# Window attention and a two-layer FFN on one core: TensorE's operands placed at multiples of 64 bytes, and the 512-column products of the second layer issued as two of 256

## The chip, the cores and the metric

The kernel runs on one core of a Trainium2 chip. The metric is the device time of one execution in microseconds (us), lower is better. The kernel before took 1079.14 us as the median of three runs (1075.65 to 1079.49).

## The reference

Windowed attention with 32 global tokens for 8 batches of 8 heads, whose output is the input of a feed-forward network with a squared ReLU. Cut to what matters:

```
s_g   = scale * q_g @ [k_g, k_l].T          # 32 global queries, 544 keys
out_g = softmax(s_g) @ [v_g, v_l]
s_l   = scale * q_l @ [k_g, k_l].T          # 512 local queries, keys within 32 places
out_l = softmax(mask(s_l)) @ [v_g, v_l]
x = concat(out_g, out_l) as (4608, 512)     # head_dim 64, 8 heads
h = x @ w_in                                # (512, 2048)
g = s * relu(h)**2 + b
out = g @ w_out                             # (2048, 512), all float32
```

## The kernel before, in words

**Precision.** A float32 operand is split into two float32r parts, a rounded one and the rest, and each product is made of three: high by high, high by low, low by high. TensorE reads 4 bytes an element in all of them.

**Attention.** Work goes in 128 steps j, one for a batch, a half of the queries and a head. The scores (`scores`, line 376) are products with 192 or 224 moving columns; `softmax` runs on VectorE and ScalarE; the probabilities are transposed on TensorE (line 317) and multiplied with the values (line 403); the global queries take lines 382, 455 and 477. The first 16 steps (`NF`) run in plain float32 on lines 283, 291, 317 and 341, while the weights of the network arrive and are split into `w_all` (lines 146 to 160).

**The network.** A tile t is 256 rows of x; 17 tiles of 8 steps make 136 steps m, and step m runs 10 steps (`LAG`) behind attention. `ffn_in` (line 525) makes two blocks of 128 hidden columns with 24 products: stationary operand 128 columns of `w_all`, moving operand 256 columns of `xs` (the split x). ScalarE and VectorE make `g` from them (lines 531 to 540). `ffn_out` (line 557) makes 12 products: stationary 128 columns of `g`, moving 512 columns of `w_all`, summed over 8 steps into two PSUM tiles `acc`. So every step m costs TensorE 24 products of 256 columns and 12 of 512, and each product loads its own stationary operand (the rows PEld of a profile).

**Order.** The program is written step by step and then put in order by the tile framework's scheduler, which goes by a simulated timeline; what stands in each engine's queue is the scheduler's choice, and small pieces of one product group can be put between two pieces of another.

**Where the operands lie.** The pools `const` and `sb` lay their tiles one behind the other in each SBUF partition, in the order of their first use, each padded to a multiple of 32 bytes. In the built program `w_all` starts at byte 2560, which is 40 times 64. Behind it the 4 bytes of `unread` take 32, and the tiles that follow start 32 bytes past a multiple of 64: `xs` at 141728 and 149920, `vs` at 158112, `sm` at 164384, `pt` at 171936, `kq` at 178592, `g` at 205344 and 209440, `qgs` at 213664, `pg` at 215712, `vsg` at 223392. Slices of these tiles start at multiples of 64 bytes from the tile's start. So each product of the network has one operand on a multiple of 64 and one off it: on line 525 the stationary `w_all` is on and the moving `xs` off, on line 557 the moving `w_all` is on and the stationary `g` off. In the products of attention (lines 376, 382, 403, 477) both operands are off. For the transposes the moving `ident` (1152) is on and the stationary `sm` off.

Of the kernel before, what the change touches and what calls it, by code (L numbers as in the profile page):

```python
# [10 lines left out]
F32 = mybir.dt.float32  # L11
F32R = mybir.dt.float32r
# [10 lines left out]
P = 128  # L23
# [49 lines left out]
def window_attention_then_ffn(ctx: ExitStack, tc: tile.TileContext, qd, qg, kw, vw, vg, qz, qgz, vz, w_in, w_out, sv, bv, out):  # L73
    nc = tc.nc
    scale = 1.0 / math.sqrt(D)

    const = ctx.enter_context(tc.tile_pool(name="const", bufs=1))
    sb = ctx.enter_context(tc.tile_pool(name="sb", bufs=2))
    ps = ctx.enter_context(tc.tile_pool(name="ps", bufs=1, space=bass.MemoryType.PSUM))

    dram = ctx.enter_context(tc.tile_pool(name="dram", bufs=1, space=bass.MemoryType.DRAM))

    ident = const.tile([P, P], F32, name="ident")
    make_identity(nc, ident)
    s_t = const.tile([P, 1], F32, name="s_t")
    b_t = const.tile([P, 1], F32, name="b_t")
# [11 lines left out]
    keep_busy(WARM_FIRST, "warm0")  # L98


    masks = {}
    for first, parts in ((True, ((32, 192, 0),)), (False, ((0, 160, 0), (192, 224, 32)))):
        mask = const.tile([P, 192 if first else 224], BF16, name=f"mask{int(first)}")
        nc.gpsimd.memset(mask, 0.0)

        for c0, c1, skip in parts:
            for sign, base in ((1, c0 - skip), (-1, 64 - c0 + skip)):
                nc.gpsimd.affine_select(
                    out=mask[:, c0:c1], in_=mask[:, c0:c1], pattern=[[sign, c1 - c0]], compare_op=ALU.is_ge,
                    fill=NEG, base=base, channel_multiplier=-sign,  # L110
                )
        masks[first] = mask


    w_all = const.tile([P, 2, 16, 2, DM], F32R, name="w_all")
    wi = w_all[:, :, :, 0].rearrange("p a f (c q) -> p a f c q", c=4)
    wo = w_all[:, :, :, 1]

# [6 lines left out]
    nc.scalar.activation(out=unread, in_=warm[:, 0:1], func=AF.Exp)  # L125

    def weight_chunk(k):
        st = sb.tile([P, 2048], I32, tag=SPOTS[k], name=f"wst{k}", bufs=2)
        n = 2 if k < BY_HALVES else 1
        sources = (w_in[k], w_out[k * P:(k + 1) * P, :])  # L130
        for i in range(2):
            queue = nc.scalar if k == 0 else nc.sync
            queue.dma_start(st[:, 1024 * i:1024 * (i + 1)], sources[i])
        for i in range(n):
            c = 1024 // n
            weight_words(k, st[:, 2 * c * i:2 * c * (i + 1)], slice(c * i, c * (i + 1)))

    def weight_words(k, st, at):
        words = st.rearrange("p (n w) -> p n w", w=2)
        low, high = words[:, :, 0], words[:, :, 1]  # L140
        n = at.stop - at.start
        parts = [slice(c, c + 512) for c in range(0, n, 512)]
        ups = []
        for h in parts:
            up = sb.tile([P, 512], I32, tag="vs", name=f"wup{k}_{at.start + h.start}", bufs=2)
            nc.scalar.activation(out=up, in_=low[:, h].bitcast(U32), func=AF.Copy, scale=2.0**-29)
            ups.append(up)
        nc.scalar.activation(out=low.bitcast(F32), in_=high.bitcast(F32), func=AF.Copy, scale=2.0**-112)  # L148
        nc.vector.tensor_scalar(
            out=low, in0=low, scalar1=3, scalar2=0x7FFFFFFF, op0=ALU.logical_shift_left, op1=ALU.bitwise_and,  # L150
        )
        for h, up in zip(parts, ups):
            nc.vector.tensor_tensor(out=low[:, h], in0=low[:, h], in1=up, op=ALU.add)  # L153
# [6 lines left out]
        nc.vector.tensor_sub(out=lo, in0=m, in1=f32(hi))  # L160
# [24 lines left out]
    def split(j):  # L185
        b, hf, h = slot(j)
        rk, rq = st_.pop(("rk", j)), st_.pop(("rq", j))
        p0 = 64 * (h % 2)
        p1 = 64 - p0
        if h % 2 == 0:  # L190
            st_["kq", j] = st_["kq", j + 1] = sb.tile([P, 2048], F32R, tag="kq", name=f"kq{j}", bufs=2)
        kq = st_.pop(("kq", j))[:, 1024 * (h % 2):1024 * (h % 2) + 1024]
        ks, qs = kq[:, 0:NC], kq[:, 512:1024].rearrange("p (i q) -> p i q", i=2)
        nc.scalar.copy(out=ks[p0:p0 + 64], in_=rk[p0:p0 + 64])  # L194
        (nc.gpsimd if K_POOL(j) else nc.vector).tensor_sub(out=ks[p1:p1 + 64], in0=rk[p0:p0 + 64], in1=f32(ks[p0:p0 + 64]))  # L195
        nc.scalar.copy(out=qs[:, 0, :], in_=rq)  # L196
        nc.gpsimd.tensor_sub(out=qs[:, 1, :], in0=rq, in1=f32(qs[:, 0, :]))  # L197
        st_["ks", j], st_["qs", j] = kq[:, 0:480], qs

    def v_split(j):  # L200
        rv = st_.pop(("rv", j))
        vs = sb.tile([P, 4, 2, D], F32R, tag="vs", name=f"vs{j}", bufs=2)
        rv4 = rv.rearrange("p (c d) -> p c d", d=D)
        nc.scalar.copy(out=vs[:, :, 0, :], in_=rv4)  # L204
        nc.gpsimd.tensor_sub(out=vs[:, :, 1, :], in0=rv4, in1=f32(vs[:, :, 0, :]))  # L205
        st_["vs", j] = vs

    def softmax(j, p_s):
        b, hf, h = slot(j)
        sm = sb.tile([P, NC], F32, tag="sm", name=f"sm{j}")  # L210
        nm = sb.tile([P, 2], F32, tag="nm", name=f"nm{j}")
        ss = sb.tile([P, 2], F32, tag="ss", name=f"ss{j}")
        cols = [COLS[hf, blk] for blk in range(2)]
        for blk in range(2):
            c = cols[blk]
            mask = masks[hf == 0 and blk == 0][:, 0:c.stop - c.start]
            nc.vector.tensor_tensor_reduce(  # L217
                out=sm[:, c], in0=p_s[:, c], in1=mask,
                op0=ALU.add, op1=ALU.min, scale=-scale, scalar=BIG, accum_out=nm[:, blk:blk + 1],
            )  # L220
        for blk in range(2):
            p = sm[:, cols[blk]]
            nc.scalar.activation(  # L223
                out=p, in_=p, func=AF.Exp, bias=nm[:, blk:blk + 1], scale=-1.0, accum_out=ss[:, blk:blk + 1],
            )
        nc.vector.tensor_scalar_add(ss, ss, 1e-9)
        nc.vector.reciprocal(ss, ss)
        for blk in range(2):
            p = sm[:, cols[blk]]
            if NORM_ACT(j):  # L230
                nc.scalar.activation(out=p, in_=p, func=AF.Copy, scale=ss[:, blk:blk + 1])  # L231
            else:
                nc.vector.tensor_scalar(  # L233
                    out=p, in0=p, scalar1=ss[:, blk:blk + 1], scalar2=1.0, op0=ALU.mult, op1=ALU.mult,
                )
        st_["p", j] = sm
# [84 lines left out]
    def transposes32(j):  # L321
        list(p_transposes(j))
        p_t = st_.pop(("pst", j))
        if j % 2 == 0:
            st_["ptp", j + 1] = sb.tile([P, 2, NC], F32, tag="pt", name=f"pt{j}")
        pt = st_["ptp", j + 1 - j % 2][:, j % 2]
        nc.scalar.copy(out=pt, in_=p_t)
        st_["pt", j] = pt
# [32 lines left out]

    def qg_split(b):
        rqg = st_["rqg", b].rearrange("p (h q) -> p h q", h=H)
        qgs = sb.tile([P, H, 2, SG], F32R, tag="qgs", name=f"qgs{b}", bufs=1)
        nc.scalar.copy(out=qgs[:, :, 0, :], in_=rqg)
        nc.gpsimd.tensor_sub(out=qgs[:, :, 1, :], in0=rqg, in1=f32(qgs[:, :, 0, :]))
        st_["qgs", b] = qgs
# [20 lines left out]

    def p_split(j):
        p_t = st_.pop(("pst", j))  # L390
        pt = sb.tile([P, 2, NC], F32R, tag="pt", name=f"pt{j}")
        nc.scalar.copy(out=pt[:, 0], in_=p_t)  # L392
        nc.vector.tensor_sub(out=pt[:, 1], in0=p_t, in1=f32(pt[:, 0]))
        st_["pt", j] = pt
# [67 lines left out]
    def g_load(b, h):  # L462
        rv = sb.tile([P, 10 * D], F32, tag="rvg", name=f"rvg{b}_{h}", bufs=1)
        nc.sync.dma_start(rv, vg[b, h // 2])
        vs = sb.tile([P, 2, 5, 2, D], F32R, tag="vsg", name=f"vsg{b}_{h}", bufs=1)
        for i in range(2):
            rv5 = rv[:, 5 * D * i:5 * D * (i + 1)].rearrange("p (c d) -> p c d", d=D)
            nc.scalar.copy(out=vs[:, i, :, 0, :], in_=rv5)  # L468
# [21 lines left out]
    xs_ = {}  # L490

    def x_split(t):
        xs = sb.tile([P, 2, 4, HALF], F32R, tag="xs", name=f"xs{t}", bufs=2)
        x = xcur.pop(t)
        for i in range(2):
            v = slice(2 * i, 2 * i + 2)
# [2 lines left out]
        xs_[t] = xs  # L499

    def xg_split(t):
        xs = sb.tile([P, 2, 4, HALF], F32R, tag="xs", name=f"xs{t}", bufs=2)
        for i in range(2):
            xr = sb.tile([P, DM], F32, tag="r", name=f"xgr{i}", bufs=2)
            nc.sync.dma_start(xr, xg_d[i * P:(i + 1) * P, :])
# [10 lines left out]
    def ffn_in(m):  # L516
# [13 lines left out]
        r = sb.tile([P, 2, HALF], F32, tag="r", name=f"r{m}", bufs=2)  # L530
        nc.scalar.activation(out=r, in_=p_h, func=AF.Relu)  # L531
        nc.vector.scalar_tensor_tensor(out=r, in0=p_h, scalar=s_t, in1=r, op0=ALU.mult, op1=ALU.mult)  # L532
        g = sb.tile([P, 2, 2, HALF], F32R, tag="g", name=f"g{m}")
        if GL_POOL(m):
            nc.vector.tensor_scalar_add(r, r, b_t)
            nc.scalar.copy(out=g[:, 0], in_=r)
# [10 lines left out]
    def ffn_out(m):  # L547
# [4 lines left out]
        for i in range(2):  # L552
            n = 0
            for k in range(2):
                f = 2 * pr + k
                for a, e in ((0, 0), (0, 1), (1, 0)):
                    nc.tensor.matmul(  # L557
                        oacc[t][i], lhsT=g[:, a, k, i * P:(i + 1) * P], rhs=wo[:, e, f, :],
                        start=(pr == 0 and n == 0), stop=(pr == 7 and n == 5),
                    )  # L560
# [169 lines left out]
```

## Time and profile before

| | |
|---|---|
| median of three runs | 1079.14 us (1075.65 to 1079.49) |
| the profiled execution | 1075.98 us, its span 1074.2 us |
| granted TensorE clock, mean | 0.985 |
| PE busy | 1034.1 us (96%), 7100 products |
| PEld busy (loads of the stationary operand) | 930.5 us (87%) |
| VectorE busy | 815.6 us (76%) |
| ScalarE busy | 726.6 us (68%) |
| GpSimd busy | 314.7 us (29%) |
| HBM traffic | 82 GB/s over the span |

The profile is one execution. PE are TensorE's products, PEld the loads of their stationary operands, DVE is VectorE, ACT ScalarE, POOL GpSimd, SP the engine that issues most transfers. A product that starts before the one ahead of it has left the array overlaps it, so its mean length is longer than its share of the time; the pace of a group is read from the starts: from the start of a group to the start of the next one, divided by the number of products. Times within the profile count from the span's start.

### The profile page before, as it was taken

Reading aid. Unit: us, or ns where it says so; the run is one execution under the profiler, and the core shown is the slowest. Engines: PE = TensorE matmul, PEld = TensorE weight load, DVE = VectorE, ACT = ScalarE, POOL = GpSimd, SP = SyncE. Lnnn points to the kernel's source line nnn. Section 1 sums busy time; section 2 is a strip of 40 time slices with the busy share of each in tenths; the row PEclk is TensorE's granted clock in tenths of the full one; section 3 lists DMA queues with packets and bytes.
Section 4 is the critical chain, followed back from the end, with each engine's and each line's share of the span. In section 5 each row is a group of like instructions: output and inputs, shape, how many; then the busy total and the mean of one; then the engine's idle time right before and its main releaser. Section 6 shows DMA issues by size and latency. Waiting matters only on the chain.

```text
span 1074.2 us, 20403 instructions
## 1 busy us (share of the span) xinstructions
PE 1034.1 (96%) x7100; PEld 930.5 (87%) x7100; DVE 815.6 (76%) x2069; ACT 726.6 (68%) x1821; POOL 314.7 (29%) x365
## 2 busy tenths in 40 slices
PE   8789779999999999999999999999999999999996
PEld 4578568999999999999999999999999999999895
DVE  5878885887879877897879887997789788963321
ACT  6898685775867776785778676876678676743221
POOL 1000161432434323442334242432344233301000
PEclk9999879999999999999999999999999999999999
DMA  7765431221313222321223131312232122201000
GB/s 258 231 192 185 144 100 49 86 76 38 101 52 101 61 66 64 92 77 46 83 69 106 38 98 55 107 57 71 59 91 77 46 89 69 68 1 47 22 20 20
DMA packets 63535, 88.89 MB, mean 83 GB/s; under 512 B 7624, under 2 KB 48584, under 8 KB 63432
## 3 DMA queue, kind: packets, MB, share of 16 engines
q1 hardware_dynamic: 63144, 86.54, 25.8%
q8 instruction: 56, 0.92, 0.3%
q10 hardware_dynamic: 288, 1.05, 0.3%
q14 instruction: 47, 0.39, 0.1%
HBM read 78.12 MB, written 9.44 MB: 82 GB/s over the span
## 4 chain that ended last, share of the span: by engine, by line
PE 81%; DVE 7%; ACT 6%; DMA 4%; issue 1%; POOL 0%; SPq 0%; ACTq 0%; POOLq 0%; DVEq 0%
PE acc L557 33%; PE ps_h L525 31%; PE ps_t L317 4%; PE ps_o L403 4%; PE ps_s L376 4%; DMA wst<-in_w_in 2%; PE ps_og L477 2%; PE ps_g L382 1%; ACT sm L223 1%; DVE sm L233 1%; DVE w_all L160 1%; DMA wst<-in_w_out 1%; DVE wst L153 1%; PE ps_tg L455 1%; ACT wst L148 1%
## 5 line engine op out<-in xcount | busy, mean ns | idle before, releaser
L525 PE MATMUL ps_h<-xs,w_all 128*128 128x256 f32 x3264 | 448.8, 284 | 8.1 <-DVE w_all L160 3.8
L525 PEld LDWEIGHTS ps_h<-xs,w_all 128*128 128x128 f32 x3264 | 417.1, 190 | 20.5 <-DVE w_all L160 4.6
L557 PE MATMUL acc<-w_all,g 128*128 128x512 f32 x1632 | 430.1, 400 | 0.4 <-ACT g L539 0.3
L557 PEld LDWEIGHTS acc<-w_all,g 128*128 128x128 f32 x1632 | 291.0, 189 | 54.8 <-ACT g L539 0.7
L197 POOL TENSOR_TENSOR kq<-rq,kq 128x256 fp32r<-128x256 f32 x112 | 98.3, 878 | 233.4 <-ACT kq L196 216.8
L205 POOL TENSOR_TENSOR vs<-rv,vs 128x256 fp32r<-128x256 f32 x112 | 85.6, 765 | 269.4 <-ACT vs L204 258.6
L532 DVE SCALAR_TENSOR_TENSOR r<-ps_h,s_t,r 128x512 f32<-128x512 f32 x136 | 101.4, 745 | 64.6 <-ACT r L531 64.5
L531 ACT ACTIVATE r<-ps_h 128x512 f32<-128x512 f32 x136 | 81.2, 598 | 86.7 <-PE ps_h L525 79.1
L223 ACT ACTIVATE sm<-sm,nm 128x224 f32<-128x224 f32 (+1 forms) x256 | 118.6, 467 | 18.9 <-DVE nm L217 17.6
L540 DVE SCALAR_TENSOR_TENSOR g<-r,b_t,g 128x512 fp32r<-128x512 f32 x136 | 106.6, 784 | 31.7 <-ACT g L539 27.5
L539 ACT ACTIVATE g<-r,b_t 128x512 fp32r<-128x512 f32 x136 | 98.7, 726 | 43.4 <-DVE r L532 42.5
L217 DVE CUSTOM_DVE_ANT_0 sm<-ps_s,mask 128x224 f32<-128x224 f32 (+1 forms) x256 | 85.3, 368 | 27.0 <-PE ps_t L317 14.8
L317 PE MATMUL ps_t<-ident,sm 128*128 128x128 f32 x512 | 95.2, 279 | 5.2 <-ACT sm L231 4.6
L233 DVE TENSOR_SCALAR sm<-sm,ss 128x192 f32<-128x192 f32 (+1 forms) x224 | 83.2, 411 | 3.3
L469 POOL TENSOR_TENSOR vsg<-rvg,vsg 128x320 fp32r<-128x320 f32 x64 | 56.8, 906 | 96.4 <-ACT vsg L468 96.3
L403 PE MATMUL ps_o<-pt,vs 128*128 128x256 f32 x448 | 84.1, 283 | 0.0
L376 PE MATMUL ps_s<-kq 128*128 128x192 f32 (+1 forms) x448 | 77.9, 279 | 5.0 <-DVE kq L195 2.7
L376 PEld LDWEIGHTS ps_s<-kq 128*128 128x128 f32 x448 | 68.8, 193 | 12.3 <-ACT sm L223 2.4
L386 ACT COPY tg<-ps_g 32x256 f32<-32x256 f32 (+1 forms) x112 | 42.3, 378 | 50.1 <-PE ps_g L382 47.6
L392 ACT CAST pt<-ps_t 128x416 fp32r<-128x416 f32 x112 | 57.3, 512 | 24.8 <-PE ps_t L317 24.1
L195 POOL TENSOR_TENSOR kq<-rk,kq 64x416 fp32r<-64x416 f32 x56 | 66.9, 1194 | 21.8 <-ACT kq L194 15.9
L403 PEld LDWEIGHTS ps_o<-pt,vs 128*128 128x128 f32 x448 | 67.6, 193 | 2.5 <-POOL vs L205 0.2
(73 smaller groups left out, 1235.0 us busy)
## 6 DMA issues: line engine op xcount, KB each, us to landing
rq<-in_qd SPq DMA_DIRECT2D x112, 128.0 KB, 2.0
rv<-in_vw SPq DMA_DIRECT2D x112, 128.0 KB, 2.0
rk<-in_kw SPq DMA_DIRECT2D x64, 208.0 KB, 2.4
rvg<-in_vg SPq DMA_DIRECT2D x32, 320.0 KB, 2.9
out<-o SPq DMA_DIRECT2D x34, 256.0 KB, 2.3
wst<-in_w_in SPq DMA_DIRECT2D x15, 512.0 KB, 4.0
wst<-in_w_out SPq DMA_DIRECT2D x15, 512.0 KB, 5.4
rv<-in_vz SPq DMA_DIRECT2D x16, 256.0 KB, 2.9
```

Of the source, the lines that this page charges most:

```text
L197: nc.gpsimd.tensor_sub(out=qs[:, 1, :], in0=rq, in1=f32(qs[:, 0, :]))
L205: nc.gpsimd.tensor_sub(out=vs[:, :, 1, :], in0=rv4, in1=f32(vs[:, :, 0, :]))
L223: nc.scalar.activation(out=p, in_=p, func=AF.Exp, bias=nm[:, blk:blk + 1], scale=-1.0, accum_out=ss[:, blk:blk + 1],)
L233: nc.vector.tensor_scalar(out=p, in0=p, scalar1=ss[:, blk:blk + 1], scalar2=1.0, op0=ALU.mult, op1=ALU.mult,)
L317: nc.tensor.transpose(out=p_t[:, at:at + P], in_=sm[:, c0:c0 + P], identity=ident)
L376: nc.tensor.matmul(p_s[:, cols], lhsT=qs[:, a, blk * P:(blk + 1) * P], rhs=ks[:, cols], start=(a == 0), stop=(a == 1),)
L403: nc.tensor.matmul(p_o[:, blk, :, q0:q0 + n], lhsT=vs[:, 2 * blk + c], rhs=pt[:, :, o], start=(c == 1), stop=(c == 0),)
L525: nc.tensor.matmul(p_h[:, k], lhsT=wi[:, a, f, c], rhs=xs[:, e, c, :], start=(n == 0), stop=(n == 11),)
L532: nc.vector.scalar_tensor_tensor(out=r, in0=p_h, scalar=s_t, in1=r, op0=ALU.mult, op1=ALU.mult)
L539: nc.scalar.activation(out=g[:, 0], in_=r, func=AF.Identity, bias=b_t)
L540: nc.vector.scalar_tensor_tensor(out=g[:, 1], in0=r, scalar=b_t, in1=f32(g[:, 0]), op0=ALU.add, op1=ALU.subtract,)
L557: nc.tensor.matmul(oacc[t][i], lhsT=g[:, a, k, i * P:(i + 1) * P], rhs=wo[:, e, f, :], start=(pr == 0 and n == 0), stop=(pr == 7 and n == 5),)
```

## The change

Three things are done.

1. A new pool `ops`, opened ahead of the others, takes the tiles that TensorE reads in the steady part: `ident`, one mask, `w_all`, `xs` (and `wst`), `vs` (and `wup`), `sm`, `pt`, `kq`, `g`, `qgs`, `vsg`. Their sizes are all multiples of 64 bytes, so in the built program all of them start at a multiple of 64: `w_all` at 2048, `xs` at 133120 and 141312, `vs` at 149504, `sm` at 153600, `pt` at 156928, `kq` at 163584, `g` at 179968 and 184064, `qgs` at 188160, `vsg` at 190208. The numbers of buffers stay what they were. The tiles left in `sb` stay 32 bytes past a multiple of 64, among them `pg` (220832), the stationary operand of line 477, and the float32 tiles `rk`, `rq`, `rv` and `sg`.
2. Each product of `ffn_out` with 512 moving columns becomes two with 256, one behind the other, with the same stationary operand; line 557 becomes line 559 and goes from 1632 products to 3264. Each of the two loads the stationary operand again.
3. As the program and its simulated times differ, the scheduler puts the instructions in another order.

```
+    ops = ctx.enter_context(tc.tile_pool(name="ops", bufs=1))
+    ident = ops.tile([P, P], F32, name="ident")
+    masks = {first: ops.tile([P, 192 if first else 224], BF16, name=f"mask{int(first)}") for first in (True,)}
+    w_all = ops.tile([P, 2, 16, 2, DM], F32R, name="w_all")
...
+    masks[False] = const.tile([P, 224], BF16, name="mask0")
...
-        vs = sb.tile([P, 4, 2, D], F32R, tag="vs", name=f"vs{j}", bufs=2)
+        vs = ops.tile([P, 4, 2, D], F32R, tag="vs", name=f"vs{j}", bufs=2)
...
-        xs = sb.tile([P, 2, 4, HALF], F32R, tag="xs", name=f"xs{t}", bufs=2)
+        xs = ops.tile([P, 2, 4, HALF], F32R, tag="xs", name=f"xs{t}", bufs=2)
...
-        g = sb.tile([P, 2, 2, HALF], F32R, tag="g", name=f"g{m}")
+        g = ops.tile([P, 2, 2, HALF], F32R, tag="g", name=f"g{m}", bufs=2)
...
                 for a, e in ((0, 0), (0, 1), (1, 0)):
-                    nc.tensor.matmul(
-                        oacc[t][i], lhsT=g[:, a, k, i * P:(i + 1) * P], rhs=wo[:, e, f, :],
-                        start=(pr == 0 and n == 0), stop=(pr == 7 and n == 5),
-                    )
+                    for z in range(2):
+                        at = slice(HALF * z, HALF * (z + 1))
+                        nc.tensor.matmul(
+                            oacc[t][i][:, at], lhsT=g[:, a, k, i * P:(i + 1) * P], rhs=wo[:, e, f, at],
+                            start=(pr == 0 and n == 0 and z == 0), stop=(pr == 7 and n == 5 and z == 1),
+                        )
                     n += 1
```

The same move from `sb` to `ops` is made for `wst`, `wup`, `kq`, `sm`, `pt`, `qgs` and `vsg`.

TensorE's queue in a step in the middle of the program, before. `ps_o` are products of probabilities and values, `ps_t` transposes, `acc_0` and `acc_1` the second layer, `ps_s` and `ps_g` scores, `ps_h` the first layer.

```order
L403 MATMUL ps_o_6055<-pt_5965,vs_5968 128x256
L403 MATMUL ps_o_6055<-pt_5965,vs_5968 128x2x96
L317 MATMUL ps_t_6058<-ident,sm_5906 128x128 x2
L403 MATMUL ps_o_6055<-pt_5965,vs_5968 128x256
L403 MATMUL ps_o_6055<-pt_5965,vs_5968 128x2x64
L317 MATMUL ps_t_6058<-ident,sm_5906 128x128 x2
L557 MATMUL acc_0_5782<-w_all,g_5948 128x512 x6
L557 MATMUL acc_1_5783<-w_all,g_5948 128x512 x6
L376 MATMUL ps_s_6096<-kq_5890 128x224 x2
L376 MATMUL ps_s_6096<-kq_5890 128x192 x2
L382 MATMUL ps_g_6101<-kq_5890,qgs_4450 64x288
L525 MATMUL ps_h_6120<-xs_5583,w_all 128x256 x24
```

And such a step of the changed kernel:

```order
L403 MATMUL ps_o_6554<-pt_6463,vs_6466 128x256
L403 MATMUL ps_o_6554<-pt_6463,vs_6466 128x2x96
L317 MATMUL ps_t_6557<-ident,sm_6404 128x128 x2
L403 MATMUL ps_o_6554<-pt_6463,vs_6466 128x256
L403 MATMUL ps_o_6554<-pt_6463,vs_6466 128x2x64
L317 MATMUL ps_t_6557<-ident,sm_6404 128x128 x2
L559 MATMUL acc_0_6361<-w_all,g_6551 128x256 x12
L559 MATMUL acc_1_6362<-w_all,g_6551 128x256 x12
L376 MATMUL ps_s_6723<-kq_6493 128x224 x2
L376 MATMUL ps_s_6723<-kq_6493 128x192 x2
L382 MATMUL ps_g_6728<-kq_6493,qgs_4885 64x288
L525 MATMUL ps_h_6747<-xs_6138,w_all 128x256 x24
```

The step keeps its order; the two rows of the second layer hold 12 products of 256 columns in place of 6 of 512.

The last steps on TensorE's queue, where attention is over, before:

```order
L525 MATMUL ps_h_13720<-xs_13423,w_all 128x256 x24
L557 MATMUL acc_0_13534<-w_all,g_13705 128x512 x6
L557 MATMUL acc_1_13535<-w_all,g_13705 128x512 x6
L525 MATMUL ps_h_13763<-xs_13423,w_all 128x256 x24
L557 MATMUL acc_0_13534<-w_all,g_13748 128x512 x6
L557 MATMUL acc_1_13535<-w_all,g_13748 128x512 x6
```

And in the changed kernel:

```order
L525 MATMUL ps_h_15319<-xs_14938,w_all 128x256 x24
L559 MATMUL acc_0_15073<-w_all,g_15292 128x256 x12
L559 MATMUL acc_1_15074<-w_all,g_15292 128x256 x12
L525 MATMUL ps_h_15374<-xs_14938,w_all 128x256 x24
L559 MATMUL acc_0_15073<-w_all,g_15347 128x256 x12
L559 MATMUL acc_1_15074<-w_all,g_15347 128x256 x12
```

Here too nothing but the shape and the number of the second layer's products moves.

More of the change, by code (lines that the diff above doesn't have):

```diff
@@ L81, in window_attention_then_ffn @@
     dram = ctx.enter_context(tc.tile_pool(name="dram", bufs=1, space=bass.MemoryType.DRAM))
-    ident = const.tile([P, P], F32, name="ident")
+    masks[False] = const.tile([P, 224], BF16, name="mask0")
     make_identity(nc, ident)
@@ L98, in window_attention_then_ffn @@
     keep_busy(WARM_FIRST, "warm0")
-    masks = {}
     for first, parts in ((True, ((32, 192, 0),)), (False, ((0, 160, 0), (192, 224, 32)))):
-        mask = const.tile([P, 192 if first else 224], BF16, name=f"mask{int(first)}")
+        mask = masks[first]
         nc.gpsimd.memset(mask, 0.0)
@@ L111, in window_attention_then_ffn @@
                 )
-        masks[first] = mask
-    w_all = const.tile([P, 2, 16, 2, DM], F32R, name="w_all")
     wi = w_all[:, :, :, 0].rearrange("p a f (c q) -> p a f c q", c=4)
@@ L127, in weight_chunk @@
     def weight_chunk(k):
-        st = sb.tile([P, 2048], I32, tag=SPOTS[k], name=f"wst{k}", bufs=2)
+        st = ops.tile([P, 2048], I32, tag=SPOTS[k], name=f"wst{k}", bufs=2)
         n = 2 if k < BY_HALVES else 1
@@ L144, in weight_words @@
         for h in parts:
-            up = sb.tile([P, 512], I32, tag="vs", name=f"wup{k}_{at.start + h.start}", bufs=2)
+            up = ops.tile([P, 512], I32, tag="vs", name=f"wup{k}_{at.start + h.start}", bufs=2)
             nc.scalar.activation(out=up, in_=low[:, h].bitcast(U32), func=AF.Copy, scale=2.0**-29)
@@ L190, in split @@
         if h % 2 == 0:
-            st_["kq", j] = st_["kq", j + 1] = sb.tile([P, 2048], F32R, tag="kq", name=f"kq{j}", bufs=2)
+            st_["kq", j] = st_["kq", j + 1] = ops.tile([P, 2048], F32R, tag="kq", name=f"kq{j}", bufs=2)
         kq = st_.pop(("kq", j))[:, 1024 * (h % 2):1024 * (h % 2) + 1024]
@@ L209, in softmax @@
         b, hf, h = slot(j)
-        sm = sb.tile([P, NC], F32, tag="sm", name=f"sm{j}")
+        sm = ops.tile([P, NC], F32, tag="sm", name=f"sm{j}", bufs=2)
         nm = sb.tile([P, 2], F32, tag="nm", name=f"nm{j}")
@@ L324, in transposes32 @@
         if j % 2 == 0:
-            st_["ptp", j + 1] = sb.tile([P, 2, NC], F32, tag="pt", name=f"pt{j}")
+            st_["ptp", j + 1] = ops.tile([P, 2, NC], F32, tag="pt", name=f"pt{j}", bufs=2)
         pt = st_["ptp", j + 1 - j % 2][:, j % 2]
@@ L363, in qg_split @@
         rqg = st_["rqg", b].rearrange("p (h q) -> p h q", h=H)
-        qgs = sb.tile([P, H, 2, SG], F32R, tag="qgs", name=f"qgs{b}", bufs=1)
+        qgs = ops.tile([P, H, 2, SG], F32R, tag="qgs", name=f"qgs{b}", bufs=1)
         nc.scalar.copy(out=qgs[:, :, 0, :], in_=rqg)
@@ L390, in p_split @@
         p_t = st_.pop(("pst", j))
-        pt = sb.tile([P, 2, NC], F32R, tag="pt", name=f"pt{j}")
+        pt = ops.tile([P, 2, NC], F32R, tag="pt", name=f"pt{j}", bufs=2)
         nc.scalar.copy(out=pt[:, 0], in_=p_t)
@@ L464, in g_load @@
         nc.sync.dma_start(rv, vg[b, h // 2])
-        vs = sb.tile([P, 2, 5, 2, D], F32R, tag="vsg", name=f"vsg{b}_{h}", bufs=1)
+        vs = ops.tile([P, 2, 5, 2, D], F32R, tag="vsg", name=f"vsg{b}_{h}", bufs=1)
         for i in range(2):
@@ L501, in xg_split @@
     def xg_split(t):
-        xs = sb.tile([P, 2, 4, HALF], F32R, tag="xs", name=f"xs{t}", bufs=2)
+        xs = ops.tile([P, 2, 4, HALF], F32R, tag="xs", name=f"xs{t}", bufs=2)
         for i in range(2):
```

## The prediction, on record before the changed kernel ran

> **What bounds the kernel now.** The first view is the page, read from the top: the busy times, the chain that ended last, and the groups.
>
> ```profile
> span 1074.2 us, 20403 instructions
> PE 1034.1 (96%) x7100; PEld 930.5 (87%) x7100; DVE 815.6 (76%) x2069; ACT 726.6 (68%) x1821; POOL 314.7 (29%) x365
> PE 81%; DVE 7%; ACT 6%; DMA 4%; issue 1%; POOL 0%; SPq 0%; ACTq 0%; POOLq 0%; DVEq 0%
> PE acc L557 33%; PE ps_h L525 31%; PE ps_t L317 4%; PE ps_o L403 4%; PE ps_s L376 4%; DMA wst<-in_w_in 2%; PE ps_og L477 2%; PE ps_g L382 1%; ACT sm L223 1%; DVE sm L233 1%; DVE w_all L160 1%; DMA wst<-in_w_out 1%; DVE wst L153 1%; PE ps_tg L455 1%; ACT wst L148 1%
> ```
>
> TensorE holds 81% of the chain, and the two layers of the network, lines 557 and 525, hold 64% of it. Whether that is so everywhere is told by the view of busy time by stretches (a stretch, its length, then PE, PEld, DVE, ACT and POOL with busy time and count, granted clock, DMA share, GB/s).
>
> ```profile
> 100.00:200.00 100.00, 84.83 (x527) 74.36 (x526) 75.77 (x167) 68.03 (x160) 30.05 (x33) 0.90 0.32 101
> 300.00:400.00 100.00, 99.73 (x715) 91.84 (x714) 82.26 (x220) 71.98 (x191) 37.01 (x42) 1.00 0.24 74
> 500.00:600.00 100.00, 99.95 (x723) 92.26 (x723) 84.85 (x224) 74.69 (x197) 40.85 (x46) 1.00 0.26 80
> 800.00:900.00 100.00, 99.94 (x714) 92.21 (x713) 82.94 (x221) 72.90 (x191) 35.92 (x42) 1.00 0.25 75
> ```
>
> In the middle TensorE never waits, at the full granted clock; VectorE, the next, is busy 82 to 85 us of 100. So there the time is the number of products by the pace of each. Up to about 160 us the weights arrive and TensorE waits; a faster product gains nothing there. The same view for lines 525 and 557 alone, from 160 us on (here only PE and PEld, in that order of lines):
>
> ```profile
> 160.00:1074.20 914.20, 411.73 (x3028) 384.12 (x3026) 1.00 0.21 65
> 160.00:1074.20 914.20, 405.02 (x1548) 275.19 (x1548) 1.00 0.21 65
> ```
>
> 3028 of 3264 and 1548 of 1632 products lie where TensorE is the bound. Their pace stands in the timeline of PE (start, length, line, count), from one start to the next.
>
> ```profile
> 1005.02 0.76 PE L477 MATMUL ps_og<-vsg,pg 128*64 128x128 f32 x10
> 1005.62 3.01 PE L557 MATMUL acc<-w_all,g 128*128 128x512 f32 x12
> ...
> 1050.34 3.02 PE L525 MATMUL ps_h<-xs,w_all 128*128 128x256 f32 x24
> 1053.20 2.96 PE L557 MATMUL acc<-w_all,g 128*128 128x512 f32 x12
> 1055.99 3.01 PE L525 MATMUL ps_h<-xs,w_all 128*128 128x256 f32 x24
> ```
>
> Line 525: (1053.20 - 1050.34) / 24 = 119.2 ns a product of 256 columns. Line 557: (1055.99 - 1053.20) / 12 = 232.5 ns for 512. Line 477: 0.60 us / 10 = 60 ns for 128. Against them stand the warm-up products in bf16, at the same granted clock:
>
> ```profile
> 21.09 1.03 PE L96 MATMUL warm<-warm 128*128 128x512 bf16 x4
> 21.95 0.60 PE L317 MATMUL ps_t<-ident,sm 128*128 128x128 f32 x4
> ```
>
> 0.86 us / 4 = 215 ns for 512 columns, 0.42 ns a column. The 4-byte products take 0.466 (line 525), 0.454 (557) and 0.469 (477). So each product of the network carries an excess that no wait of the profile explains: 119.2 - 107.5 = 11.7 ns on line 525, and 17.5 ns on line 557. What the change is worth hangs on whether placement is the cause of this excess.
>
> **The change part by part.** *The split.* If a column costs what it does now, two products of 256 stand in place of one of 512. At the pace of line 525 that is 2 x 119.2 - 232.5 = 5.9 ns for each of 1632, 9.6 us. The low end comes from the short products: two of 128 at 60 ns cost 0.8 ns more than one of 256, and 0.8 x 1632 is 1.3 us. I take the middle, 5.5 us. The Trainium skill, page TensorE: Matmul & The Clock Gate, section Back-to-back issue gap, gives a warm product N / 2.4 + 2.5 ns. By it a second product costs 2.5 ns, 4.1 us in all, and a 256-column one would take 109.2 ns; the bf16 row agrees (215.8 by the rule, 215 measured), the 4-byte rows do not.
>
> The second load of the same stationary operand lies beside the first half's columns as long as loads come faster than products. The scores on line 376 show how fast they come:
>
> ```profile
> 711.73 0.58 PE L376 MATMUL ps_s<-kq 128*128 128x224 f32 x4
> 712.15 0.29 PE L382 MATMUL ps_g<-kq,qgs 128*64 128x288 f32 x1
> 712.29 3.01 PE L525 MATMUL ps_h<-xs,w_all 128*128 128x256 f32 x24
> ```
>
> Four products, each with a load of 128 columns, in 0.42 us: 105 ns a product. Loads are the bound there, since 192 to 224 columns need less, and 105 is under 119 and under 107.5. So the 1632 added loads are covered; if that cover were gone, 256-column products could not fall below about 105 ns.
>
> *The placement.* No row of before shows a 4-byte product with both operands on a multiple of 64 bytes, so its worth is bounded from both sides. One end: the whole excess goes. Then lines 525 and 559 run at 107.5 ns; 11.7 x 3028 = 35.4 us and 17.5 x 1548 = 27.1 us, together 62.5 us. The other end: nothing, because three products with different operands off the grid have nearly the same time a column. Below nothing I see no reason to go: line 477, with both operands at the same place in the 64 bytes, is no slower a column than line 525, where they differ.
>
> Between the ends I take a mechanism that can be counted. A row of 256 columns that starts 32 bytes off the grid covers 17 pieces of 64 bytes in place of 16. If the array is fed by such pieces, one of sixteen goes with the change: 107.5 / 16 = 6.7 ns a product. The product of 256 columns would then take 119.2 - 6.7 = 112.5 ns, on line 525 and on line 559 alike. That is 6.7 x 3028 = 20.3 us, and 232.5 - 2 x 112.5 = 7.5 ns for each of 1548, 11.6 us; together 31.9 us, the split's price included. This lies at half of the upper end. What speaks against it is line 557, whose moving operand is on the grid and which has an excess all the same; the mechanism needs the load of the misplaced `g` to disturb the stream there.
>
> What is late next: a step of the middle shrinks by 24 x 6.7 + 12 x 7.5 = 251 ns. It runs from the transposes' end to the same place a step later, about 7 us:
>
> ```profile
> 708.85 3.04 PE L557 MATMUL acc<-w_all,g 128*128 128x512 f32 x12
> 715.89 3.05 PE L557 MATMUL acc<-w_all,g 128*128 128x512 f32 x12
> ```
>
> 7.04 us, so TensorE becomes 3.6% faster and VectorE's share rises from 82 to 85 us of 100 to 85 to 88. That is still no bound, but VectorE and ScalarE hand work to TensorE in chains; I give back a tenth, 3 us. The products of attention keep their time: lines 376, 403 and the transposes go by loads. The scheduler's new order moves nothing within a step but the shape of the second layer's products, and I cost it at nothing: where TensorE never waits, the order of its products does not change their sum. If that cover is gone, in the first 160 us, some us either way.
>
> Sum on the profiled execution: its 1074.2 us of span and 1.8 us around it make 1075.98; less 31.9, plus 3, is 1047 us. The median of the runs shown is 3 us above the profiled execution, so a median near 1050 would fit as well.
>
> **The rivals.** *The whole excess goes.* Then 62.5 us fall off TensorE, a step shrinks by 24 x 11.7 + 12 x 17.5 = 491 ns of 7040, 7%, and VectorE stands at 88 to 91 us of 100. Loads at 105 ns and the chains through VectorE begin to bind; I give back 15 us. 1076 - 62.5 + 15 is 1028 us. For it: bf16 runs at 215 ns under the same clock. Against it: a 4-byte column brings twice the bytes, which alone may cost the excess.
>
> *The placement does nothing, and the split is nearly free.* All three combinations in the trace, stationary on and moving off (0.466 ns a column), moving on and stationary off (0.454), both off (0.469), go at nearly one pace; a cost of each misplaced operand would add up in the last, and it does not. Then the excess belongs to the 4-byte stream, and the time is 1076 plus 1.3 to 5 us, about 1079. The Trainium skill speaks for this: the page SBUF — State Buffer, section Specifications (TRN2), gives lines of 16 bytes, at least two accesses to a line for full bandwidth and a penalty at each new one. Every operand here starts on a multiple of 16 already, so by that rule nothing is gained by 64; the equal paces above agree.
>
> *Slower: the placement does nothing, and the split costs what line 525 costs.* Place: the second layer's 12 products of a step, everywhere where TensorE is the bound. Price: 5.9 ns for each 512 columns, up to 9.6 us; with 7 to 9.6 us it is 1083 to 1086 us. It decides as soon as the placement saves less than about 0.7 ns a product: the 9.6 us less the 5.4 us that a measurement can tell, over the 6292 products of 256 columns from 160 us on (3028 and 2 x 1548) is 0.67.
>
> **How the numbers follow.** A time within 0.5% (5.4 us) of before is what a measurement of this kernel cannot tell from no change; the three runs spread over 0.36%. The forecast, with part of the excess gone (1036 to 1067), gets 0.41. The whole excess gone (1020 to 1036) gets 0.15: both have the unexplained excess for them. Nothing from the placement gets 0.44, because the one test that the trace holds is against an effect of each operand alone; I divide it into 0.20 for the nearly free split and 0.24 for the dear one. So faster is 0.41 + 0.15 = 0.56, same 0.20, slower 0.24. The likeliest single case gives 1047 us, with 1036 to 1067 its own range. The range that holds eight times in ten must reach into the cases on both sides: from 1023, within the case of the whole excess, to 1085, within that of the dear split.
>
> **What would show it.** In the profile of the changed kernel the timeline of PE after 1000 us has line 525 and line 559 alone: 24 products from start to start in 2.70 us would be the forecast (112.5 ns each), 2.58 the whole excess, and 2.86 no effect of the placement. Line 559's 24 halves are to be read beside the 2.79 us of before: 2.80 to 2.86 is the split without any gain. If both layers stand at 2.86 us, the forecast is wrong, and the cause is that the excess is of the 4-byte stream. If they shrink and the time does not, the busy time of PE by stretches will have fallen under 99 of 100, with VectorE or ScalarE named in the chain.

## The result: 1.3% slower, and the profile after

The changed kernel takes 1091.17 us (median of 6 runs, 1089.70 to 1093.72) against 1076.85 us for the kernel before in 6 runs beside it: ratio 1.0126, 95% interval 1.0110 to 1.0142, or 14.3 us. One execution of a later run (xs_apart) had a granted clock of 0.556, took 1678.26 us, and is left out of that run's ratio. The profiled execution has a span of 1087.9 us, 13.7 more than before. The page after, in the same places as before:

```profile
span 1087.9 us, 23685 instructions
PE 1049.7 (96%) x8730; PEld 1024.2 (94%) x8732; DVE 821.7 (76%) x2069; ACT 727.9 (67%) x1821; POOL 309.9 (28%) x365
PE acc L559 34%; PE ps_h L525 33%; PE ps_t L317 5%; PE ps_s L376 4%; PE ps_o L403 4%; DMA wst<-in_w_in 2%; PE ps_og L477 2%; PE ps_g L382 1%; DMA wst<-in_w_out 1%; ACT wst L148 1%; DVE wst L153 1%; ACT wup L146 1%; DVE w_all L160 1%; PE ps_tg L455 1%; ACT w_all L159 1%
```

TensorE's share is still 96%, and the chain is the same; only loads of stationary operands went from 87% to 94%. By stretches (columns as in the prediction):

```profile
300.00:400.00 100.00, 100.00 (x868) 100.00 (x867) 82.71 (x221) 72.92 (x191) 36.26 (x42) 1.00 0.24 74
800.00:900.00 100.00, 100.00 (x861) 99.82 (x860) 83.31 (x221) 71.52 (x186) 34.20 (x40) 1.00 0.23 71
```

No new wait shows in these stretches: TensorE works all the time at the full granted clock, and VectorE stands where it stood. So the 14 us are a slower pace of products. The timeline of PE, a step in the middle and three groups at the end (start, length, line, count):

```profile
702.87 3.11 PE L559 MATMUL acc<-w_all,g 128*128 128x256 f32 x24
...
710.02 3.12 PE L559 MATMUL acc<-w_all,g 128*128 128x256 f32 x24
...
1055.24 3.04 PE L559 MATMUL acc<-w_all,g 128*128 128x256 f32 x24
1058.12 3.04 PE L525 MATMUL ps_h<-xs,w_all 128*128 128x256 f32 x24
1061.00 3.04 PE L559 MATMUL acc<-w_all,g 128*128 128x256 f32 x24
```

The step in the middle takes 7.15 us in place of 7.04. At the end both layers stand at 2.88 us for 24 products, 120.0 ns each, group after group, where line 525 had 2.86 and line 557 2.79. From 160 us on, where TensorE is the bound, the kernel before has 129 groups of the second layer (1548 / 12) and 126 of the first (3028 / 24). That gives 0.09 x 129 = 11.6 us and 0.02 x 126 = 2.5 us, an estimate of 14.1 in all; the span grew by 13.7 and the median by 14.3.

### The profile page after: what moved, and what is told of

Its sections match the earlier page's. It is cut to its first block, busy times and chain, and to the rows that moved or that the text cites. A ratio compares the mean times of both kernels' runs of the same rounds, so it can differ in the third digit from the quotient of the medians.

```text
span 1087.9 us, 23685 instructions
## 1 busy us (share of the span) xinstructions
PE 1049.7 (96%) x8730; PEld 1024.2 (94%) x8732; DVE 821.7 (76%) x2069; ACT 727.9 (67%) x1821; POOL 309.9 (28%) x365
## 4 chain that ended last, share of the span: by engine, by line
PE 85%; ACT 5%; DMA 4%; DVE 4%; issue 1%; POOL 0%; SPq 0%; POOLq 0%; ACTq 0%; DVEq 0%
PE acc L559 34%; PE ps_h L525 33%; PE ps_t L317 5%; PE ps_s L376 4%; PE ps_o L403 4%; DMA wst<-in_w_in 2%; PE ps_og L477 2%; PE ps_g L382 1%; DMA wst<-in_w_out 1%; ACT wst L148 1%; DVE wst L153 1%; ACT wup L146 1%; DVE w_all L160 1%; PE ps_tg L455 1%; ACT w_all L159 1%
## 5 line engine op out<-in xcount | busy, mean ns | idle before, releaser
L525 PE MATMUL ps_h<-xs,w_all 128*128 128x256 f32 x3264 | 438.0, 286 | 6.2 <-DVE w_all L160 2.7
L559 PE MATMUL acc<-w_all,g 128*128 128x256 f32 x3264 | 442.5, 287 | 0.1
L525 PEld LDWEIGHTS ps_h<-xs,w_all 128*128 128x128 f32 x3264 | 410.7, 192 | 8.4 <-DVE w_all L160 3.4
L559 PEld LDWEIGHTS acc<-w_all,g 128*128 128x128 f32 x3264 | 409.4, 192 | 0.5 <-ACT g L539 0.3
L540 DVE SCALAR_TENSOR_TENSOR g<-r,b_t,g 128x512 fp32r<-128x512 f32 x136 | 113.0, 831 | 25.3 <-ACT g L539 17.3
L217 DVE CUSTOM_DVE_ANT_0 sm<-ps_s,mask 128x224 f32<-128x224 f32 (+1 forms) x256 | 85.6, 366 | 11.6 <-PE ps_s L376 7.7
L233 DVE TENSOR_SCALAR sm<-sm,ss 128x192 f32<-128x192 f32 (+1 forms) x224 | 75.2, 378 | 3.5
L376 PE MATMUL ps_s<-kq 128*128 128x192 f32 (+1 forms) x448 | 69.4, 276 | 7.1 <-DVE nm L217 4.7
L226 DVE TENSOR_SCALAR ss<-ss 128x2 f32<-128x2 f32 x128 | 28.6, 224 | 56.4 <-ACT sm L223 55.9
L393 DVE TENSOR_TENSOR pt<-ps_t,pt 128x416 fp32r<-128x416 f32 x112 | 65.5, 585 | 7.3 <-ACT pt L392 6.4
L376 PEld LDWEIGHTS ps_s<-kq 128*128 128x128 f32 x448 | 61.5, 195 | 7.7 <-POOL kq L195 2.6
```

Of the source, the lines that this page charges most:

```text
L217: nc.vector.tensor_tensor_reduce(out=sm[:, c], in0=p_s[:, c], in1=mask, op0=ALU.add, op1=ALU.min, scale=-scale, scalar=BIG, accum_out=nm[: ...
L376: nc.tensor.matmul(p_s[:, cols], lhsT=qs[:, a, blk * P:(blk + 1) * P], rhs=ks[:, cols], start=(a == 0), stop=(a == 1),)
L525: nc.tensor.matmul(p_h[:, k], lhsT=wi[:, a, f, c], rhs=xs[:, e, c, :], start=(n == 0), stop=(n == 11),)
L540: nc.vector.scalar_tensor_tensor(out=g[:, 1], in0=r, scalar=b_t, in1=f32(g[:, 0]), op0=ALU.add, op1=ALU.subtract,)
L559: nc.tensor.matmul(oacc[t][i][:, at], lhsT=g[:, a, k, i * P:(i + 1) * P], rhs=wo[:, e, f, at], start=(pr == 0 and n == 0 and z == 0), stop ...
```

## The experiments

A pace below is read as in the prediction, from start to start of a group in the last steps, where attention is over and the groups are long. Timed kernels come with their ratio to the kernel before and its interval; the others with the time of one execution, which bears no verdict by itself. Where an edit adds lines, lines 525 and 559 appear as 526 and 560, and 557 as 558.

### Placement and split apart

Two theories stood. S: placement is worth nothing, the split costs. P: on the grid a 4-byte stream is slower.

**on_whole**, the placement alone. Edit to the changed kernel:

```
-                    for z in range(2):
...
+                    nc.tensor.matmul(
+                        oacc[t][i], lhsT=g[:, a, k, i * P:(i + 1) * P], rhs=wo[:, e, f, :],
```

> The new placement alone: every operand on a multiple of 64 bytes, the second layer's products whole (512 columns), the order of before. Theory S (the split is what costs, placement is worth nothing): 512-column products stay at 232.5 ns, line 525 at 119.2, time 1075 to 1079 us. Theory P (on the 64-byte grid a 4-byte stream loses one column's time in nine, so 0.469 ns a column, and off it a little less): 512-column products take 240 ns, line 525 exactly 120, time about 1088 to 1092 us.

Ratio 0.9986 (0.9973 to 0.9999), 1075.49 us. Its timeline of PE:

```profile
1044.81 2.91 PE L557 MATMUL acc<-w_all,g 128*128 128x512 f32 x12
1047.56 3.04 PE L525 MATMUL ps_h<-xs,w_all 128*128 128x256 f32 x24
1050.43 2.91 PE L557 MATMUL acc<-w_all,g 128*128 128x512 f32 x12
```

Line 557 takes 2.75 / 12 = 229.2 ns, 3.3 less than before, line 525 2.87 / 24 = 119.6. The time is the one that S gave, and P's is refuted for whole products. But neither theory has these paces: whole products gain with the new placement, and those of 256 columns do not.

**mixed_halves**, the split alone: the kernel before with the loop over z of the changed one.

> The split alone: the placement of before, each 512-column product as two of 256, the order of the changed kernel. Theory S: two halves at 119 to 120 ns each, time 1086 to 1092 us. Theory P: halves at 117 to 118 ns like the clean runs of line 525 before, time 1077 to 1082 us.

Ratio 1.0040 (1.0028 to 1.0052), 1081.46 us. Its timeline of PE:

```profile
1047.82 3.00 PE L559 MATMUL acc<-w_all,g 128*128 128x256 f32 x24
1050.66 2.98 PE L525 MATMUL ps_h<-xs,w_all 128*128 128x256 f32 x24
1053.48 3.00 PE L559 MATMUL acc<-w_all,g 128*128 128x256 f32 x24
```

Halves at 2.84 / 24 = 118.3 ns, line 525 at 117.5. The split alone costs 4 us, in P's bounds and outside S's. So -1.5 us and +4.3 us alone, +14 together: the two parts don't add up. TensorE's queue has the same order in this kernel and the changed one, so the order is not the cause.

**off_whole** and **off_halves** put `w_all` and every tile behind it 32 bytes further, by making the mask ahead of `w_all` 32 bytes longer. Both operands of each product of the network then lie 32 bytes past a multiple of 64. The order on TensorE's queue is that of the runs on the grid; off_whole has whole products, as on_whole.

```
-    masks = {first: ops.tile([P, 192 if first else 224], BF16, name=f"mask{int(first)}") for first in (True,)}
+    masks = {first: ops.tile([P, 208 if first else 224], BF16, name=f"mask{int(first)}") for first in (True,)}
```

> All operands of the pool, the weights too, 32 bytes past a multiple of 64; products whole. Theory S: as before, 1075 to 1079 us. Theory P: no product is on the grid, so none is slower than before; 512 columns at 232.5 ns or less, time 1070 to 1077 us. If what counts is that both operands lie at the same place within 64 bytes, it is as slow as with both on the grid.

> All operands 32 bytes past a multiple of 64, and the second layer's products as two of 256. Theory S: like the changed kernel, 1088 to 1093 us, halves at 120 ns. Theory P: halves at 117 to 118 ns, 1076 to 1082 us. If the same place within 64 bytes is what counts, 120 ns as in the changed kernel.

off_whole: ratio 0.9992 (0.9982 to 1.0001), 1076.35 us, and in the timeline of PE 228.3 and 119.6 ns, near the paces of on_whole:

```profile
1045.30 3.04 PE L525 MATMUL ps_h<-xs,w_all 128*128 128x256 f32 x24
1048.17 2.91 PE L557 MATMUL acc<-w_all,g 128*128 128x512 f32 x12
1050.91 3.04 PE L525 MATMUL ps_h<-xs,w_all 128*128 128x256 f32 x24
```

off_halves: 1.0126 (1.0113 to 1.0139), 1090.93 us, the changed kernel's ratio to the digit. Its timeline of PE:

```profile
1055.98 3.04 PE L559 MATMUL acc<-w_all,g 128*128 128x256 f32 x24
1058.86 3.04 PE L525 MATMUL ps_h<-xs,w_all 128*128 128x256 f32 x24
1061.74 3.04 PE L559 MATMUL acc<-w_all,g 128*128 128x256 f32 x24
```

Again 120.0 ns. P falls here, as S fell with mixed_halves. Both operands off the grid give what both on it give, so the multiple of 64 is not what counts. What these two share, and the kernel before has not, is that moving and stationary operand lie alike within 64 bytes.

### Is it the load of the next stationary operand?

The load runs beside the stream, so three theories were set against each other: L (the load takes time from the stream, 13 ns for 128 columns), B (the load is the bound), S (the stream is slow in proportion to its columns; not the S of above). Three kernels cut one of the two, in the changed kernel; a fourth narrows the load beside whole products. In all four, and in two_bytes below, the scheduler's order in earlier steps differs from that of the kernel edited, so the paces at the end are compared and not the times.

```
+                    cut = P if n in (0, 11) else 64
                     nc.tensor.matmul(
-                        p_h[:, k], lhsT=wi[:, a, f, c], rhs=xs[:, e, c, :],
+                        p_h[0:cut, k], lhsT=wi[:, a, f, c, 0:cut], rhs=xs[:, e, c, :],
```

**narrow_load**:

> The changed kernel, but in the first layer 10 of the 12 products that are summed into a block load 64 stationary columns in place of 128 (half of their hidden columns are left out); 256 columns stream as before. Theory L (the load of the next stationary operand takes time from the stream that runs beside it, in proportion to its columns, 13 ns for 128): line 525 at about 113 ns a product in its long groups. Theory B (a product waits for its load, and a load of 128 columns takes 120): about 109, the bf16 pace. Theory S (a 4-byte stream is slow by itself, in proportion to its columns): 120 as in the changed kernel.

**narrow_stream**, with `cut = HALF if n == 0 else 240` on the columns of `xs`:

> The changed kernel, but 11 of the 12 products of the first layer's sums stream 240 columns in place of 256 (the last 16 rows of x are left out of them); loads stay at 128 columns. Theory L: 240 / 2.4 + 13.3 is about 113 ns a product. Theory S: 120 x 240 / 256 is 112.5. Theory B: 120 ns, unchanged, since the load sets the pace.

**narrow_load_32**:

> As the run with 64 stationary columns in the first layer, with 32 in their place (three quarters of the hidden columns are left out of 10 of 12 products). If the load's cost goes with its columns: 106.7 + 3.3, so 110 ns a product on line 526, after 120 with 128 columns and 114 with 64. If half of the saving with 64 columns came from another cause, 113 to 114 as there.

**whole_narrow_load**, the same cut on `g` in the run with the placement alone:

> The new placement with whole products, but 94 of the 96 products that are summed into an output block load 64 stationary columns of g in place of 128 (half of the rows of the output are left out of them); 512 columns stream. If the excess of a whole product is its load's too: 213.3 + 6.7, so 220 ns in the settled runs in place of 227. If the excess goes with the 512 streamed columns: 227 as without it.

One execution each: 1076.57, 1069.10, 1080.86 and 1073.29 us. In this order, from the timeline of PE of each (a row names the shape of its first product, so narrow ones stand under 128\*128 and 128x256 in the first three):

```profile
1039.63 2.92 PE L526 MATMUL ps_h<-xs,w_all 128*128 128x256 f32 x24
1042.39 3.04 PE L560 MATMUL acc<-w_all,g 128*128 128x256 f32 x24
```

```profile
1038.05 2.87 PE L526 MATMUL ps_h<-xs,w_all 128*128 128x256 f32 x24
1040.76 3.03 PE L560 MATMUL acc<-w_all,g 128*128 128x256 f32 x24
```

```profile
1043.69 2.99 PE L526 MATMUL ps_h<-xs,w_all 128*128 128x256 f32 x24
1046.52 3.04 PE L560 MATMUL acc<-w_all,g 128*128 128x256 f32 x24
```

```profile
1045.02 2.92 PE L558 MATMUL acc<-w_all,g 128*64 128x512 f32 x12
1047.78 3.02 PE L525 MATMUL ps_h<-xs,w_all 128*128 128x256 f32 x24
```

With 64 columns loaded, 20 products of 24 are narrow; with 120 ns for the other 4 they take (2760 - 480) / 20 = 114 ns, as L said. With 32, L asks for 110, and (2830 - 480) / 20 = 117.5 came. Beside 512 columns L asked for 220, and 2.76 / 12 = 230 came, more than the 229.2 with the full load. So L fell: the pace does not go with the columns loaded. B fell too, since a quarter of the load leaves 117.5, and since with 240 streamed columns (22 of 24) the pace is (2710 - 240) / 22 = 112.3 under the full load. S and L both fit that last run (112.5 and 113), but S asked for 120 with 64 columns loaded, where 114 came, so S fell as well. That load and stream disturb each other in a way that does not go with the load's length is not excluded by these runs.

**two_bytes** reads the second layer's operands as bf16, at the same addresses:

```
-                            oacc[t][i][:, at], lhsT=g[:, a, k, i * P:(i + 1) * P], rhs=wo[:, e, f, at],
+                            oacc[t][i][:, at], lhsT=g2[:, a, k, i * P:(i + 1) * P, 1], rhs=wo2[:, e, f, at, 1],
```

> The changed kernel, but the second layer reads only the upper two bytes of each number of g and w_all as bf16 (the rest of each number is left out), at the same addresses, every second two-byte word; 256 columns a product, one load each. If the excess belongs to four-byte operands, line 560 goes at 108 to 110 ns a product. If it belongs to the bytes that a column lies apart in memory, it stays at 120 or gets slower.

One execution: 1072.98 us, and in the timeline of PE:

```profile
1041.72 3.11 PE L525 MATMUL ps_h<-xs,w_all 128*128 128x256 f32 x24
1044.68 2.90 PE L560 MATMUL acc<-w_all,g 128*128 128x256 bf16 x24
1047.32 3.11 PE L525 MATMUL ps_h<-xs,w_all 128*128 128x256 f32 x24
```

2.64 / 24 = 110 ns, at the upper edge of what the first case asked for, but the group ahead shows 2.96 in place of 2.88, so some of that is a shift of the border; with line 525 at 120 the pair's 5.60 us leave 2.72 / 24 = 113.3 for line 560. The last group, 48 products with none behind them, has no such border. Here it is in the changed kernel and in two_bytes:

```profile
1072.52 5.92 PE L559 MATMUL acc<-w_all,g 128*128 128x256 f32 x48
1055.88 5.61 PE L560 MATMUL acc<-w_all,g 128*128 128x256 bf16 x48
```

The difference of 0.31 us over 47 spacings is 6.6 ns, so 113.4 after 120.0, and within the groups of two_bytes, behind the first product, the starts of single products are 113 and 114 ns apart. So 6.7 ns of the 12.5 over 107.5 go with the width of the operands, of load and stream together; the other 5.8 ns two-byte operands have as well, at least with the columns 4 bytes apart as here.

### How the operands lie to each other

Four kernels move `w_all` against the other operands, in the changed kernel:

```
-    w_all = ops.tile([P, 2, 16, 2, DM], F32R, name="w_all")
+    w_room = ops.tile([P, 64 * DM + 32], F32R, name="w_all")
+    w_all = w_room[:, 16:16 + 64 * DM].rearrange("p (a f e d) -> p a f e d", a=2, f=16, e=2)
```

with 16, 4 and 1 elements (64, 16 and 4 bytes), and later with none. The new tile is 128 bytes longer than `w_all`, so in all four every tile behind it lies 128 bytes further than in the changed kernel, which the first three expectations leave out. The run with none, apart_128, has this shift by itself, and the other three are to be compared with it.

> The changed kernel with w_all alone moved by 64 bytes, so that in both layers the two operands of a product are 64 bytes apart within 128 and at one place within 64. If the place within 64 bytes is what counts, all groups stay at 120 ns a product and the time at 1088 to 1093 us. If the place within 128 counts, they go to 117 to 118 ns and 1079 to 1083 us, as in the split alone.

> The changed kernel with w_all alone moved by 16 bytes. If any difference within 64 bytes breaks the even pace, 117 to 118 ns a product and 1079 to 1083 us; if it takes a difference of 32, 120 ns and 1088 to 1093 us. It tells what the grid of the effect is.

> The changed kernel with w_all alone moved by 4 bytes, off every grid but its own elements. If pieces of 16, 32 or 64 bytes are fetched whole and a row that starts off them needs one more, the loads and the second layer's streams get slower, over 120 ns a product. If only the relation of the two operands counts, 117 to 120 ns.

> The changed kernel with everything behind w_all moved by 128 bytes, so that the operands of a product keep their place within 128 but not within 256. If the place within 128 bytes is what counts: 120 ns a product and 1088 to 1093 us, as in the changed kernel. If it is the place within 256 or more, another pace.

Times in this order: 1072.80, 1086.12, 1097.14 (kernel before 1077.55) and 1087.33 us (1076.93); TensorE's queue has the changed kernel's order in all four. From the timeline of PE in apart_64 and in apart_4:

```profile
1044.74 2.90 PE L560 MATMUL acc<-w_all,g 128*128 128x256 f32 x24
1047.47 2.88 PE L526 MATMUL ps_h<-xs,w_all 128*128 128x256 f32 x24
1050.19 2.99 PE L560 MATMUL acc<-w_all,g 128*128 128x256 f32 x24
1053.02 2.99 PE L526 MATMUL ps_h<-xs,w_all 128*128 128x256 f32 x24
1055.85 5.61 PE L560 MATMUL acc<-w_all,g 128*128 128x256 f32 x48
```

```profile
1062.53 3.11 PE L560 MATMUL acc<-w_all,g 128*128 128x256 f32 x24
1065.48 3.01 PE L526 MATMUL ps_h<-xs,w_all 128*128 128x256 f32 x24
1068.33 3.11 PE L560 MATMUL acc<-w_all,g 128*128 128x256 f32 x24
```

With the operands 64 bytes apart both layers run at 113.8 and 113.3 ns in one step and at 117.9 in the next, in the same program with the same shapes; 4 bytes apart, line 560 takes 122.9 and line 526 118.8. In apart_16 both lie at 118.3 to 118.8, and its time falls between its two cases. So the same product has paces from 113 to 123 ns, and the distance of its operands moves them. The starts of single products in the traces tell an even pace from a mean: in the groups at the end of the changed kernel every spacing is 120 ns, and those of apart_64, but for the first ones of a group, are 113 and 114 in one step and 117 to 119 in the next; but the 118.3 of mixed_halves is a mean of spacings of mostly 115 to 123, and the 122.9 of apart_4 of spacings from 119 to 127. The 64-byte case of equal place is refuted: 64 apart is alike within 64 and not at 120. In apart_128 the groups are at 2.84 to 2.86 us, 118 to 119 ns, not locked at 120; that its time of 1087.33 is near the changed kernel's doesn't make its pace the same, so a place within 128 bytes does not tell all either:

```profile
1050.31 3.02 PE L526 MATMUL ps_h<-xs,w_all 128*128 128x256 f32 x24
1053.17 3.01 PE L560 MATMUL acc<-w_all,g 128*128 128x256 f32 x24
1056.01 3.00 PE L526 MATMUL ps_h<-xs,w_all 128*128 128x256 f32 x24
```

**halves_64** is apart_64 timed again in five executions, **whole_64** the same distance with whole products.

> The run with w_all moved by 64 bytes and halves once more, timed in rounds: 1071 to 1075 us, faster than the kernel before by 0.3 to 0.5%, if the one look was no accident; 1088 to 1092 us if it was.

> The new placement with w_all moved by 64 bytes, so that the two operands of each product of the network lie 64 bytes apart within 128, and the second layer's products whole. If a load costs the stream 6.7 ns in place of 13.3 where the operands lie 64 apart: line 525 at 113 to 116 ns, line 557 at 220 to 224, time 1045 to 1060 us. If only halves gain by it: 1070 to 1076 us.

halves_64: ratio 0.9956 (0.9942 to 0.9970), 1072.16 us: a split kernel can be faster than before. whole_64: 1.0001 (0.9989 to 1.0013), 1076.76 us; its timeline of PE:

```profile
1042.64 2.96 PE L558 MATMUL acc<-w_all,g 128*128 128x512 f32 x12
1045.44 2.99 PE L526 MATMUL ps_h<-xs,w_all 128*128 128x256 f32 x24
1048.27 2.96 PE L558 MATMUL acc<-w_all,g 128*128 128x512 f32 x12
```

Line 558 stands at 233.3 ns, no better than before, and line 526 at 117.9: the first case did not come, and the time lies 0.8 us over the second. What is good for halves is not for whole products.

**xs_apart** takes for each layer what the earlier runs had best: `g` and `w_all` on multiples of 64, `xs` back in the old pool, 32 bytes past one, products whole, the order of before. The tiles through which the weights arrive in the place of `xs` go back with it.

```
-        xs = ops.tile([P, 2, 4, HALF], F32R, tag="xs", name=f"xs{t}", bufs=2)
+        xs = sb.tile([P, 2, 4, HALF], F32R, tag="xs", name=f"xs{t}", bufs=2)
```

> Whole products of 512 columns, g and w_all on multiples of 64, xs alone 32 bytes past one: second layer at one place within the 64 bytes, first layer apart, the order of before. If the relation of the two operands of a product sets its pace: line 557 at 227 ns in its settled runs as in the run with the new placement alone, line 525 at 118 as before, time 1071 to 1075 us, under both. If what was gained there came from elsewhere: 1075 to 1078 us.

> The kernel of the run with xs alone apart, once more, for a profile at the full clock: line 557 at 227 ns in its settled runs and line 525 at 118, time 1072 to 1076 us.

1074.01 us, ratio 0.9969 (0.9957 to 0.9980), and in the second run 1073.25 us, 0.9953 (0.9933 to 0.9972): faster than both kernels. The pace is read from the second run, in its timeline of PE:

```profile
1045.12 2.89 PE L557 MATMUL acc<-w_all,g 128*128 128x512 f32 x12
1047.85 3.02 PE L525 MATMUL ps_h<-xs,w_all 128*128 128x256 f32 x24
1050.70 2.89 PE L557 MATMUL acc<-w_all,g 128*128 128x512 f32 x12
```

227.5 ns on line 557 and 118.8 on line 525, near what on_whole (229.2) and the kernel before (119.2) have for these relations.

## Why the prediction was wrong, step by step

**What bounds the kernel: right.** TensorE stays busy 100 of 100 us in the stretches shown, and the slower pace of lines 525 and 559 (14.1 us) accounts for the time.

**The split: right in size by itself.** 1.3 to 9.6 us were given; alone it measures 1.0040, 4.3 us. **The cover of the added loads: not refuted, but its number is off.** No run shows a load as the bound: with a quarter of the columns loaded the pace goes from 120.0 to 117.5 only, though with half of them it is 114. The 105 ns on line 376 is the spacing of the products; in the trace the starts of the loads in that group are 109 and 111 ns apart, so at the 107.5 ns of the prediction's other end they would not have been covered.

**The placement: this step failed.** It read "A row of 256 columns that starts 32 bytes off the grid covers 17 pieces of 64 bytes in place of 16", 6.7 ns saved on each product of lines 525 and 559. On line 525 the pace went from 119.2 to 120.0 ns, and off_halves, where all operands are off the grid, has the same 120.0. Being on the grid is not what counts. What counts is how the two operands of a product lie to each other: with halves, from 32 bytes apart to alike, the time goes from 1081.46 (mixed_halves) to 1091.17 us. The prediction set the other end of the bound at nothing, because "line 477, with both operands at the same place in the 64 bytes, is no slower a column than line 525"; that compared 128 columns and 64-column loads with 256 and 128, and was no test of this. The true end was below nothing: with the operands alike, halves take 120.0 ns where the split alone has 118.3. That is 3.4 ns for each pair, line 525 goes from 117.5 to 120.0 between the same runs, and it comes on top of the split's price. The far end, 107.5 ns, was half of a bf16 product of 512 columns; the one bf16 row with 256, in two_bytes, has 113.3. One count is off and changes nothing: from 160 us on there are 3028 + 2 x 1548 = 6124 products of 256 columns, not 6292, so the 0.67 ns is 0.69.

**The rivals.** The dear split had the sign and the place right. It priced a pair at 2 x 119.2; 2 x 120.0 came, 7.5 ns more than the 232.5 of the whole product in place of 5.9, and line 525 paid 0.8 ns too, which it left out; hence 14.3 us in place of 9.6. That it came so near was partly luck: its premise, that the placement does nothing, is refuted, and the split by itself, which it priced at 7 to 9.6 us, costs 4.3. The free split assumed no effect of the placement, which the runs refute: on_whole and mixed_halves alone sum to about 3 us, the changed kernel has 14. The whole excess gone has no run for it: no product of 256 columns settles under 113.3 ns. The sign that was named for a wrong forecast, both layers at 2.86 us, nearly came with 2.88, but it was to mean that the placement has no effect, and it has one.

**The rule of 16-byte lines**, in the Trainium skill's page SBUF — State Buffer, section Specifications (TRN2), was read as nothing to be gained by 64, and off_halves agrees: the same 1.0126 on the grid and off it. But lines of 16 bytes do not cover how two operands lie to each other: moving `w_all` by 64 bytes, a multiple of 16, against the rest takes 1087.33 us (apart_128) to 1072.16 (halves_64).

**What stays open.** What sets the pace of a product is not settled. The theories that its load takes the time, or its columns alone, fell. The paces that were seen can be ordered: the fastest settled ones are 113.3 ns for 256 columns and 227.5 for 512. They lie near 17/16 of N / 2.4; with the N / 2.4 of the Trainium skill's page TensorE: Matmul & The Clock Gate, section Back-to-back issue gap, that is 113.3 and 226.7, an estimate. The 113.3 is no mark of four-byte operands, since two_bytes has it too. Above the fastest paces a product carries between nothing and about 7 ns more, up to 120.0 and 233.3. Read so, the split costs what its second product carries: all of it in the changed kernel, little in halves_64. This fits these rows, but no run isolates its cause. The 122.9 ns in apart_4 lie outside it, and neither why the groups alternate in apart_64 nor why operands alike give 120.0 in the changed kernel and off_halves but 118 to 119 in apart_128 was found.

## What to carry to other kernels

Before splitting products or moving tiles for TensorE, time the pair of changes apart: here each was nearly free alone and the two together cost 1.3%. A product's pace, read from start to start in a stretch without waits, shows such an effect to a nanosecond, and it depended on how moving and stationary operand lie to each other, not on a multiple of 64 for either. A mechanism that explains one line should be asked for the other one before it is priced: the second layer's moving operand was on the grid all along and had the excess.

## What the runs showed of the hardware that was not expected

Float32r products of one shape have several paces at the full granted clock: 113.3 and 117.9 ns for 256 columns within one program (apart_64) and 120.0 in others, 227.5 to 233.3 for 512, against 215 ns for 512 in bf16. Moving one operand by 4, 16 or 64 bytes, with TensorE's queue in the same order, gave 1097, 1086 and 1073 us, and 1087 without the move. PEld near 100% does not tell how fast the products go: from 300 to 400 us it is busy 100 of 100 us both in the changed kernel, with 868 products, and in halves_64, with 891.
